# Denominators before numerators, and a fused bf16 weight, in a linear-attention kernel

## The chip, the cores and the metric

The kernel runs on one core of a Trainium2 chip. The metric is the device time in microseconds of one execution. TensorE multiplies matrices into PSUM banks of 512 fp32 columns; ScalarE and VectorE read PSUM and work in SBUF; SyncE (SP) issues DMAs; all engines run their own queues in program order and wait for each other by semaphores.

## The reference

The layer-normalised input (2048 tokens of 512, bf16) feeds two branches, whose sum is added to the input. The first is linear attention with 32 heads of 16:

```
phi = concat(softmax(p), softmax(-p))        # p = q @ w_phi or k @ w_phi, per head
kv  = sum over s of phi_k[s] (x) v[s];  z = sum over s of phi_k[s]
num = phi_q @ kv;  den = phi_q . z + 1e-6
branch_A = (num / den) @ wo
branch_B = mish(xn @ w1 + b1) @ w2           # 1792 hidden columns
out = x + branch_A + branch_B
```

## The kernel before

Tokens are worked in 16 tiles of 128, in groups of four. The first half of the program (to about 99 us) makes the layer norm, keys, values and the hidden layer; the second makes the query side, both second matmuls and the output. The order is written out by hand and kept, so each engine's queue is the program's order.

The query softmaxes are not normalised on their own: `exponentials` leaves exp of both signs ("planes") in `e`, and `turn` transposes it by DMA into `qT`. A pair h of two tiles then goes through these steps, i being the tile in the pair:

- `attend(h, i)` (L324) multiplies `qT` by the masked `kvm` in 32 small matmuls (L337) into `pnd`, four PSUM banks of which there is one set. For each of two planes and each head it holds 16 numerators, and for each pair of heads (a row block r and a column block j of 36 columns) four further columns: two denominators and two sums of the plane (the softmax denominators of the exponentials). ScalarE copies the numerators to SBUF as bf16 (L347; into the tiles `wkp` and `wv`, free by then) and the four columns as fp32 to `ds` (L348).
- `combine(h, parts)` (L350) works on VectorE on one tile (a slice of one) or both. It crosses each plane's denominator with the other plane's sum (`u`, L370), adds the two planes (`w`, L373), takes the reciprocal (L376), multiplies it by the other plane's sum to get each plane's weight (L379), and copies that to bf16 twice side by side (`f`, L382), because the product with the numerators (L389) then reads pairs of bf16. L396 adds the planes into `ob`, and L399 lets SP transpose it by DMA.
- `second_layer(t)` (L415) accumulates the second branch in `po`; `project_out(h)` (L424) adds the transposed `ob` times `wo` to the same bank, and `residual` (L432) adds the input and frees the bank.

The second half calls these steps interleaved, with `extremes` (L225 to L234: VectorE's maximum and minimum of each head), `exponentials` (L244, ScalarE) and `logits` (L168, copied at L209) of the next group between them. `combine` is called with single tiles for h = 0, 2, 3, 4 and 7, with both for h = 1, 5 and 6: 13 parts in all.

Of the kernel before, what the change touches and what calls it, by code (L numbers as in the profile page):

```python
# [10 lines left out]
FP32 = mybir.dt.float32  # L11

ACT = mybir.ActivationFunctionType
ALU = mybir.AluOpType
# [4 lines left out]
def kernel(  # L19
# [12 lines left out]
    nc = tc.nc  # L32
    P = 128
# [25 lines left out]
    opool = ctx.enter_context(tc.tile_pool(name="opool", bufs=2))  # L59
# [264 lines left out]
    def attend(h, i):  # L324

        if i == 0:
            nd_of[h] = (
                (wkp, wv)[h % 2][:].rearrange("p (i l) c -> p i l c", i=2),
                opool.tile([P, 2, 2, 4, 4, 4], FP32, name="ds"),
            )  # L330
        nm, ds = nd_of[h]
        pnd = later[0].tile([P, 4, 512], FP32, name="pnd", tag="nd")
        for pl in range(2):
            for j in range(4):
                for r in range(4):
                    at, rows = (pl * 4 + j) * 36, slice(32 * r, 32 * r + 32)
                    nc.tensor.matmul(  # L337
                        pnd[:, r, at : at + 36],
                        lhsT=qT_of[h][rows, i, pl * 4 + j, :],
                        rhs=kvm[rows, pl, j, :],  # L340
                        start=True,
                        stop=True,
                        tile_position=(32 * r, 0),
                    )
        a = pnd[:, :, 0:288].rearrange("p r (l j c) -> p l j r c", l=2, j=4)
        to = nm[:, i, :, :].rearrange("p l (j r c) -> p l j r c", j=4, r=4)
        nc.scalar.copy(to, a[:, :, :, :, 0:32])  # L347
        nc.scalar.copy(ds[:, i], a[:, :, :, :, 32:36])  # L348

    def combine(h, parts=(slice(0, 2),)):  # L350

        nm, ds = nd_of.pop(h) if parts[-1].stop == 2 else nd_of[h]
        ds = ds[:].rearrange("p i l j r (x h) -> p i l x (j r) h", x=2)
        if h not in oT_of:
            ob = lnp.tile([P, 4, 512], BF16, name="ob", tag="xn")
            u = opool.tile([P, 2, 2, 32], FP32, name="u")
            w = opool.tile([P, 2, 32], FP32, name="w")
            f = opool.tile([P, 2, 2, 32, 2], BF16, name="f")
            tmp_of[h] = ob[:, 0:2, :], u, w, f
            oT_of[h] = ob[:, 2:4, :].rearrange("p i (j c) -> p (i j) c", c=P)  # L360
        o_t, u, w, f = tmp_of[h]
        for q in parts:
            n = q.stop - q.start
            uh = u[:, q].rearrange("p i l (c h) -> p i l c h", h=2)
            wh = w[:, q, None, :].to_broadcast([P, n, 2, 32]).rearrange(
                "p i l (c h) -> p i l c h", h=2
            )
            for i in range(n):
                k = q.start + i
                nc.vector.tensor_tensor(  # L370
                    out=uh[:, i], in0=ds[:, k, :, 0], in1=ds[:, k, ::-1, 1], op=ALU.mult
                )
            nc.vector.tensor_tensor(  # L373
                out=w[:, q], in0=u[:, q, 0, :], in1=u[:, q, 1, :], op=ALU.add
            )
            nc.vector.reciprocal(w[:, q], w[:, q])  # L376
            for i in range(n):
                k = q.start + i
                nc.vector.tensor_tensor(  # L379
                    out=uh[:, i], in0=ds[:, k, ::-1, 1], in1=wh[:, i], op=ALU.mult  # L380
                )
            nc.vector.tensor_copy(  # L382
                f[:, q].rearrange("p i l c o -> p (i l c) o"),
                u[:, q].rearrange("p i l (c o) -> p (i l c) o", o=1).to_broadcast(
                    [P, n * 64, 2]
                ),
            )
            v = nm[:, q].rearrange("p i l (c e o) -> p (i l c) e o", e=8, o=2)
            nc.vector.tensor_tensor(  # L389
                out=v, in0=v,  # L390
                in1=f[:, q].rearrange("p i l c o -> p (i l c) o")[:, :, None, :].to_broadcast(
                    [P, n * 64, 8, 2]
                ),
                op=ALU.mult,
            )
            nc.vector.tensor_tensor(  # L396
                out=o_t[:, q], in0=nm[:, q, 0, :], in1=nm[:, q, 1, :], op=ALU.add
            )
            nc.sync.dma_start_transpose(  # L399
                out=oT_of[h][:, 4 * q.start : 4 * q.stop, :],  # L400
                in_=o_t[:, q].rearrange("p i c -> p (i c)"),
            )
# [55 lines left out]
    for sign in (1, -1):  # L458
        nc.gpsimd.affine_select(
            out=block[:], in_=block[:], pattern=[[-16 * sign, 8], [0, 16]],  # L460
# [9 lines left out]
    for _ in range(12):  # L470
# [7 lines left out]
        out=Wbd[:].rearrange("p j (h e) -> p j h e", h=8),  # L478
        in0=block[:, None, :, :].to_broadcast([P, 4, 8, 16]),
        in1=wsrc[:, :, None, :].to_broadcast([P, 4, 8, 16]),  # L480
        op=ALU.mult,
# [90 lines left out]
    hidden(2)  # L572
    second_layer(1, 0, 2)
    attend(0, 0)
    second_layer(1, 2, 12)
    attend(0, 1)
    extremes(5, halves=low)
    second_layer(1, 12)
    combine(0, first)
    combine(0, last)  # L580
    extremes(5, halves=high)
    exponentials(5, (0,))
    second_layer(2)
    attend(1, 0)
    second_layer(3)
    attend(1, 1)
    project_out(0)
    combine(1)
    store()
    for i in range(TPG):  # L590
# [92 lines left out]
```

## Time and profile before

| | |
|---|---|
| median of 3 runs | 181.95 us (181.59 to 182.17) |
| profiled execution | 181.76 us, span 179.8 us |
| granted TensorE clock | 0.997 |
| TensorE, VectorE, ScalarE busy | 170.8, 154.0, 123.9 us |
| numerators L347, denominators L348 (ScalarE) | 16 of 1.01 us, 16 of 0.27 us |
| `u` L370, `w` L373, reciprocal L376 (VectorE), one tile | 0.22, 0.19, 0.35 us |
| L379, `f` L382, L389, L396 (VectorE), one tile | 0.22, 0.23, 0.69, 0.42 us |
| DMA transposes of `ob` L399 | 13, median 2.5 us from issue to landing |

The span runs from the first instruction to the last; the rest of the execution's time lies around it. A wait is put down to whatever released the waiting instruction. A busy matmul is not a matmul at its peak: its end is modelled, so that matmuls are better counted by the pitch from one start to the next.

### The profile page before, as it was taken

The page shows a single profiled execution, that of the slowest core. Times are in us where ns is not written, and L with a number is a line of the kernel's source. Part 1 is how long each engine was busy: PE and PEld are TensorE (multiplying, and loading weights), DVE is VectorE, ACT ScalarE, POOL GpSimd, SP SyncE. Part 2 cuts the span into 40 slices and gives each one's busy share as a digit, 9 for nine tenths or more (in the row PEclk, how much of TensorE's full clock was granted, in tenths as well). Part 3 has the DMA queues.
Part 4 walks back from the last instruction along what each step waited for, and adds up shares of the span by engine and source line. Part 5 has one row for each costly group of instructions (what it writes and reads, how often), then busy time and mean ns, then how long its engine had stood idle before and what let it go on. Part 6 is the DMA issues. An engine that isn't in the chain of part 4 may idle for free.

```text
span 179.8 us, 4310 instructions
## 1 busy us (share of the span) xinstructions
PE 170.8 (95%) x1785; PEld 81.8 (46%) x1807; DVE 154.0 (86%) x313; ACT 123.9 (69%) x162; POOL 29.6 (16%) x42
## 2 busy tenths in 40 slices
PE   6799999999999999999999999899999999998993
PEld 2454443454444545544454444344444444443561
DVE  1989979997999989998999959799899978798853
ACT  2367999999998899969994987379223863543200
POOL 4404069400799300000000000000000000000000
PEclk9999999999999999999999999999999999999998
DMA  5997796300023600000000692809945078386334
GB/s 145 295 400 277 165 343 180 69 5 4 4 53 64 120 0 4 0 4 0 0 4 0 129 108 60 120 5 145 227 115 99 0 136 130 88 86 154 62 91 142
DMA packets 44527, 18.12 MB, mean 101 GB/s; under 512 B 36956, under 2 KB 43996, under 8 KB 44508
## 3 DMA queue, kind: packets, MB, share of 16 engines
q1 hardware_dynamic: 43536, 17.50, 44.4%
q10 hardware_dynamic: 972, 0.35, 0.7%
q8 instruction: 14, 0.23, 0.5%
q14 instruction: 5, 0.04, 0.1%
HBM read 6.84 MB, written 2.10 MB: 50 GB/s over the span
## 4 chain that ended last, share of the span: by engine, by line
DVE 47%; PE 33%; ACT 8%; DMA 8%; issue 2%; DVEq 0%; ACTq 0%; SPq 0%
PE po L415 14%; DVE s L262 7%; DVE m L225 6%; PE po L424 6%; PE ph L189 6%; PE pproj L168 5%; ACT e L244 5%; DVE stats L128 5%; DVE e L234 5%; DVE e L275 4%; DMA ob<-ob 4%; DVE r L270 3%; DMA qT<-e 2%; DVE x_sb L432 2%; DMA x_sb<-in_A_x_dram 2%
## 5 line engine op out<-in xcount | busy, mean ns | idle before, releaser
L415 PE MATMUL po<-w_sb,acts 128*128 128x512 bf16 (+1 forms) x224 | 50.2, 366 | 0.8 <-PE pnd L337 0.2
L189 PE MATMUL ph<-xnT,w_sb 128*128 128x512 bf16 x224 | 49.5, 379 | 0.4 <-ACT acts L196 0.4
L196 ACT ACTIVATE acts<-ph,b1f 128x512 bf16<-128x512 f32 x56 | 34.7, 705 | 2.0 <-PE ph L189 1.9
L244 ACT ACTIVATE e<-e 128x2048 bf16<-128x2048 bf16 x16 | 30.2, 1911 | 6.5 <-DVE e L234 6.4
L189 PEld LDWEIGHTS <-w_sb 128*128 128x128 bf16 x224 | 21.8, 98 | 26.8 <-issue 0.7
L415 PEld LDWEIGHTS <-acts 128*128 128x128 bf16 x238 | 22.2, 98 | 22.5
L168 PEld LDWEIGHTS <-xnT 128*128 128x128 bf16 x192 | 18.2, 98 | 22.0 <-DMA xnT<-xn 0.8
L262 DVE TENSOR_REDUCE s<-e 128x128 f32<-128x2048 bf16 x8 | 18.2, 2278 | 2.5 <-ACT e L244 2.5
L347 ACT CAST wv<-pnd 128x1024 bf16<-128x1024 f32 x8 | 8.1, 1010 | 14.5 <-PE pnd L337 12.3
L140 POOL TENSOR_SCALAR xn<-x_sb,mv,rstd 128x512 bf16<-128x512 bf16 x8 | 16.7, 2102 | 0.2
L424 PE MATMUL po<-wqk,ob 128*128 128x512 bf16 (+1 forms) x67 | 15.1, 367 | 1.3 <-DMA ob<-ob 1.2
L432 DVE TENSOR_TENSOR x_sb<-po,x_sb 128x512 bf16<-128x512 f32 (+1 forms) x17 | 11.0, 658 | 5.7 <-PE po L424 5.7
L168 PE MATMUL pproj<-wv,xnT 128*128 128x512 bf16 x61 | 14.8, 380 | 0.2
L209 ACT CAST p_sb<-pproj 128x512 bf16<-128x512 f32 x21 | 11.3, 587 | 4.9 <-PE pproj L168 4.9
L168 PE MATMUL pproj<-wqk,xnT 128*128 128x512 bf16 x62 | 14.4, 379 | 0.3 <-DVE x_sb L432 0.2
L225 DVE TENSOR_TENSOR m<-m 128x256 bf16<-128x256 bf16 (+2 forms) x44 | 13.4, 305 | 1.5
L128 DVE BATCH_NORM_STATS2 stats<-x_sb 128x6 f32<-128x512 bf16 x16 | 10.0, 680 | 3.8 <-DMA x_sb<-in_A_x_dram 3.8
L168 PE MATMUL pproj<-wkp,xnT 128*128 128x512 bf16 x50 | 11.8, 379 | 0.1
L347 ACT CAST wkp<-pnd 128x1024 bf16<-128x1024 f32 x8 | 8.1, 1014 | 3.5 <-PE pnd L337 3.4
L275 DVE TENSOR_TENSOR e<-e,r 128x2048 bf16<-128x2048 bf16 x8 | 10.3, 1282 | 0.3
L424 PEld LDWEIGHTS <-ob 128*128 128x128 bf16 x68 | 6.4, 98 | 8.3 <-DMA ob<-ob 1.8
L225 DVE TENSOR_TENSOR m<-p_sb 128x1024 bf16<-128x1024 bf16 (+1 forms) x18 | 10.2, 565 | 0.0
(66 smaller groups left out, 170.2 us busy)
## 6 DMA issues: line engine op xcount, KB each, us to landing
w_sb<-in_B_w_dram SPq DMA_DIRECT2D x2, 1792.0 KB, 8.9
out_dram<-x_sb SPq DMA_DIRECT2D x15, 128.0 KB, 1.9
x_sb<-in_A_x_dram SPq DMA_DIRECT2D x1, 1024.0 KB, 11.4
x_sb<-in_A_x_dram SPq DMA_DIRECT2D x1, 512.0 KB, 4.4
wv<-in_A_wqkv_dram SPq DMA_DIRECT2D x1, 512.0 KB, 5.2
wqk<-in_A_wo_dram SPq DMA_DIRECT2D x1, 512.0 KB
x_sb<-in_A_x_dram SPq DMA_DIRECT2D x1, 256.0 KB, 3.0
x_sb<-in_A_x_dram ACTq DMA_DIRECT2D x1, 256.0 KB, 3.3
```

The costliest lines, as they stand in the source:

```text
L128: nc.vector.bn_stats(stats[:, i, :], x_sb[:, t0 + i, :])
L140: engine.tensor_scalar(out=xn[:, at + i, :], in0=x_sb[:, t0 + i, :], scalar1=mv[:, i, 0:1], scalar2=rstd[:, i : i + 1], op0=ALU.subtract, ...
L168: nc.tensor.matmul(pp, lhsT=xnT[:, t, kt, :], rhs=w[:, kt, :], start=(kt == 0), stop=(kt == KT - 1),)
L189: nc.tensor.matmul(ph[:], lhsT=w1_sb[:, kt, f * P : (f + 1) * P], rhs=xnT[:, g * TPG : (g + 1) * TPG, kt, :], start=(kt == 0), stop=(kt == ...
L196: nc.scalar.activation(acts[:, f, g * 512 : (g + 1) * 512], ph[:], ACT.Mish, bias=b1f[:, f : f + 1])
L225: nc.vector.tensor_tensor(out=m, in0=src[:, :, 0:half], in1=src[:, :, half : 2 * half], op=op)
L244: nc.scalar.activation(v, v, ACT.Exp)
L262: nc.vector.reduce_sum(t[:], v.rearrange("p t l (c e) -> p (t l c) e", e=16), axis=AX.X)
L275: nc.vector.tensor_tensor(out=vv, in0=vv, in1=r2[:, :, None, :].to_broadcast([P, 128, 8, 2]), op=ALU.mult)
L347: nc.scalar.copy(to, a[:, :, :, :, 0:32])
L415: nc.tensor.matmul(po[:, c], lhsT=acts[:, f, t * P : (t + 1) * P], rhs=w2_sb[:, f, c], start=(f == 0), stop=False,)
L424: nc.tensor.matmul(po[:, c], lhsT=oT_of[h][:, t % 2 * 4 + j, :], rhs=wo_sb[:, j, c], start=False, stop=(j == 3),)
```

## The change

In `attend`, ScalarE copies the four columns first and the numerators second. The columns are laid out by plane of meaning: `ds` is now (tile, denominators or sums, 64), where it was (tile, plane, j, r, 4). In `combine`, `u` for two tiles is one instruction instead of two. The multiplication that gives each plane's weight writes bf16 pairs directly into `f`, reading both its fp32 operands with each element twice, one instruction for each tile; the separate copy into `f` is gone.

```
@@ attend
-                opool.tile([P, 2, 2, 4, 4, 4], FP32, name="ds"),
+                opool.tile([P, 2, 2, 64], FP32, name="ds"),
...
+        nc.scalar.copy(
+            ds[:, i].rearrange("p x (g r h) -> p g r x h", g=8, r=4),
+            pnd[:, :, 0:288].rearrange("p r (g c) -> p g r c", g=8)[:, :, :, 32:36].rearrange(
+                "p g r (x h) -> p g r x h", x=2
+            ),
+        )
         nc.scalar.copy(to, a[:, :, :, :, 0:32])
-        nc.scalar.copy(ds[:, i], a[:, :, :, :, 32:36])
@@ combine
-        ds = ds[:].rearrange("p i l j r (x h) -> p i l x (j r) h", x=2)
+        ds = ds[:].rearrange("p i x (l c) -> p i x l c", l=2)
...
-            for i in range(n):
-                k = q.start + i
-                nc.vector.tensor_tensor(
-                    out=uh[:, i], in0=ds[:, k, :, 0], in1=ds[:, k, ::-1, 1], op=ALU.mult
-                )
+            nc.vector.tensor_tensor(
+                out=u[:, q], in0=ds[:, q, 0], in1=ds[:, q, 1, ::-1], op=ALU.mult
+            )
             nc.vector.tensor_tensor(
                 out=w[:, q], in0=u[:, q, 0, :], in1=u[:, q, 1, :], op=ALU.add
             )
             nc.vector.reciprocal(w[:, q], w[:, q])
-            for i in range(n):
-                k = q.start + i
+            for k in range(q.start, q.stop):
                 nc.vector.tensor_tensor(
-                    out=uh[:, i], in0=ds[:, k, ::-1, 1], in1=wh[:, i], op=ALU.mult
+                    out=f[:, k],
+                    in0=ds[:, k, 1, ::-1, :, None].to_broadcast([P, 2, 32, 2]),
+                    in1=w[:, k, None, :, None].to_broadcast([P, 2, 32, 2]),
+                    op=ALU.mult,
                 )
-            nc.vector.tensor_copy(
-                f[:, q].rearrange("p i l c o -> p (i l c) o"),
-                u[:, q].rearrange("p i l (c o) -> p (i l c) o", o=1).to_broadcast(
-                    [P, n * 64, 2]
-                ),
-            )
```

## The prediction

> **What bounds the kernel now.** I read the page first: engine shares and the chain that ended last.
>
> ```profile
> PE 170.8 (95%) x1785; PEld 81.8 (46%) x1807; DVE 154.0 (86%) x313; ACT 123.9 (69%) x162; POOL 29.6 (16%) x42
> ...
> DVE 47%; PE 33%; ACT 8%; DMA 8%; issue 2%; DVEq 0%; ACTq 0%; SPq 0%
> ```
>
> TensorE is busy for 95% of the span, yet VectorE holds 47% of the chain. So the end is set by TensorE's list of matmuls plus the few places where that list waits, and a faster VectorE is worth only what those places lose. All instructions that the diff touches run after 102 us, so next I asked for the waits after 99 us (waiter, what it waited for: us in total, times, longest).
>
> ```profile
> DVE u L370 <- ACT ds L348: 2.3, 2, 1.9
> PEld L424 <- DMA ob<-ob: 1.8, 2, 1.1
> PE po L424 <- DMA ob<-ob: 1.2, 2, 0.6
> ...
> PE pproj L168 <- DVE x_sb L432: 0.2, 1, 0.2
> ```
>
> TensorE waits in the output projection (L424) for the transposed product twice, and once for a residual (L168 behind L432). The chain of waits shows how the first L424 wait comes about.
>
> ```profile
> 103.98 0.90 ACT wkp L347
> 104.88 0.18 ACT ds L348
> ...
> 106.47 0.70 DVE wkp L389
> ...
> 110.11 4.20 DMA ob<-ob
> 114.30 0.05 issue
> 114.35 1.04 PE po L424 x4
> ```
>
> ScalarE copies numerators, then denominators; VectorE, idle for 1.88 us by then, starts L370 at 105.08 and reaches L389 at 106.47, and from there to TensorE at 114.35 nothing else decides. The timeline gives the size of each wait and the two older chains.
>
> ```profile
> 112.70 1.04 PE L424 MATMUL po<-wqk,ob 128*128 128x512 bf16 x4
> 114.35 1.04 PE L424 MATMUL po<-wqk,ob 128*128 128x512 bf16 x4 [0.61 <-DMA ob<-ob]
> ...
> 136.26 3.61 PE L168 MATMUL pproj<-wqk,xnT 128*128 128x512 bf16 x16 [0.15 <-DVE x_sb L432]
> ...
> 158.94 0.36 DVE L379 TENSOR_TENSOR u<-ds,w 128x64 f32<-128x64 f32 x2
> ...
> 164.82 1.90 PE L424 MATMUL po<-wqk,ob 128*128 128x512 bf16 x8 [0.59 <-DMA ob<-ob]
> ```
>
> A busy matmul row includes its modelled tail, so I size waits by pitch. Undisturbed, 14 matmuls of 512 columns and one attend repeat every 3.43 us; 0.30 of that is the attend, so the pitch is 0.215 us. At 112.70 four matmuls end their slots at 113.56, and the next starts at 114.35: **0.79 us** lost. At 135.73 the first weights of L168 load, and undisturbed the matmul follows some 0.21 later; it starts at 136.26: **0.31 us** lost. At 163.85 an attend starts, 0.30 later L424 could; it starts at 164.82: **0.67 us** lost. Together 1.77 us.
>
> **The change, part by part.** *The copies' order.* ScalarE's pair costs the same: 1.01 and 0.27 us, the second starting about 0.15 before the first ends (104.76 against 103.87 + 1.01). The bank group pnd, of which there is one, is therefore released when it was, so the next attend does not wait longer. Denominators now end at about 103.87 + 0.27 = 104.14 instead of 105.05, numerators at about 105.04 instead of 104.88. The second is late only for whoever has nothing to do before needing them, and VectorE still has its chain ahead of L389: the added wait there is covered by that chain (1.19 us, below) against 0.90 us of numerators left. Without that cover it would cost at most 0.15 us.
>
> *The copy's layout.* The read order is as before, the writes now go in pairs of fp32 elements, the x planes 64 elements apart. No ScalarE row shows such a write. Lower bound 271 ns (L348 as it is; 1024 elements cost 1012, so time goes by the element, and a gain has nowhere to come from); upper bound twice that, 0.54 us. I take 0.27, because on VectorE the old L370 read in pairs at 218 ns, while L373 on 64 contiguous elements takes 225. At 0.54 the first chain below gains 1.02 instead of 1.29 us, still over what it needs.
>
> *VectorE, a part with one half (10 of 13).* Start to start in the first combine: u to w 0.26, w to reciprocal 0.23, reciprocal to u 0.38, u to f 0.26, f to L389 0.26: 1.39 us. The last two steps become one fp32 product of 128 elements. The trace has no such row: L373 costs 192 ns on 32 elements and 225 on 64, so 1.03 ns each, and 128 give 225 + 66 = 291. The floor is the cast's 227, the ceiling the reciprocal's slope (353 at 32, 554 at 64, 6.3 ns each), 0.96 us; it is a multiply with fp32 operands, so I take 0.29, with 0.03 to the next. The chain becomes 0.26 + 0.23 + 0.38 + 0.32 = 1.19 us: 0.20 saved.
>
> *A part with both halves (3 of 13).* In combine(5) L370 starts at 157.70, L373 at 158.09, L379 at 158.94, L389 at 159.66. One u on 128 elements takes 0.29 + 0.03, so 0.06 saved. The pair L379 takes 0.36 for two of 0.22, so the second adds 0.14; a pair of products of 0.29 then takes 0.29 + 0.21 + 0.03 = 0.53, against 0.72 from L379 to L389: 0.19 saved. Together 0.25 us.
>
> The Trainium skill ("VectorE: DVE Perf Modes", "The DRAIN you can't avoid") says the next instruction does not start until the pipe has emptied and that chaining doesn't avoid this, with earlier starts only for instructions that are not held. Taken strictly, the pair of products would cost 0.09 more and the whole sum below would be 1.2 us; the pair of 0.36 us for two of 0.22 is against it here.
>
> *Where it falls on the path.* Wait one: L389 of combine(0, first) moves from 106.47 to 104.19 + 1.19 = 105.38, 1.09 earlier (numerators are there at 105.04); the second part adds 0.20, so its transpose is issued 1.29 earlier, at 108.82, and lands near 113.0, before 113.56. All **0.79** are gained; late next is nothing, since the following residuals wait on TensorE itself. Wait two: VectorE runs without a gap from the residual at 127.55 through combine(2, last) and both parts of combine(3), so it is 0.6 earlier at the residual, which then waits for its matmuls: L424 at 134.21 plus the 1.06 that a residual follows at elsewhere (125.62 to 126.68) is 135.27 instead of 135.52: **0.25**. Wait three: the chain is residual at 157.09 (after TensorE), combine(5), transpose, L424; it shortens by **0.25** and stays the later one, with 0.42 left. The other combines have cover: their projections start with no wait. At the end, L424 runs through from 172.94 with no wait, so the tail gives nothing. SP issues the same transposes in the same order; the two qT transposes at 111.35, which queued behind ob's issue, move forward with it.
>
> Sum: 0.79 + 0.25 + 0.25 = 1.29 us. The profiled execution took 181.76 (span 179.8 and 1.96 around it), so 180.47; the median of the runs is 0.19 above it, so 180.66. I say 180.6.
>
> **Rivals.** *Only the first wait goes* (18%): waits two and three hang on residuals that follow TensorE and on a transpose that takes 3.08 us behind a qT transpose; if queueing eats the 0.25s, the gain is 0.79 and the time 181.15. For it: that landing is over the median of 2.5. Against it: qT there also follows VectorE's e, so it moves too.
>
> *Transposes land when the queue lets them* (12%): the first took 4.20 us, beside two qT transposes. If they fix its landing, the first gain is also lost: 181.7 to 181.95. Against it: qT's issue came after ob's, in order on SP.
>
> *The fused product is slow* (8%): two operands, each read twice over, one reversed by planes. Let it cost x more than 0.29. Then wait one gains 1.29 - 2x, at most 0.79; wait two 0.6 - 3x, at most 0.25; wait three 0.25 - 2x. The sum turns negative at x = 0.31, a product of 0.60 us; at the ceiling, x = 0.66, it is -0.03 - 1.38 - 1.07 = -2.5 us: 184.4. Against it: the cast L382 already repeats each element, at 227 ns.
>
> That the denominators do not come first cannot be, the queue being in program order.
>
> **How the numbers follow.** All three waits shrink: 62%, its own range 180.3 to 181.0 (0.35 either side of 180.66, half again the 0.25 of a smaller wait). A measurement here can tell about 0.3%, 0.55 us, from no change, so faster means under 181.40. The first case and nearly all of the second are: 0.79. Within: 0.14 (the third and the edge of the second). Slower: 0.07. The range runs from 180.1 (all 1.77 us of waits gone from the median, 180.18) to 181.7 (the second case, 181.15, with the 0.55 on top); the slow product and most of the third case lie outside.
>
> **What would show it.** Right: ds before the numerators, at 0.27 us; VectorE's idle before u at 104.2; a product near 0.29 us, and 1.19 from u to L389; no wait at the second L424 group, 0.4 us at the one near 164, none at L168 near 135; TensorE's idle after 99 us down by about 1.3. Wrong: a product over 0.6 us, a ds copy over 0.5, or transposes landing where they did though issued 1.3 earlier.

## The result and the profile after

The changed kernel takes 180.68 us (median of 6 runs, 180.49 to 180.89) against 182.12 for the kernel before beside it: ratio 0.9922, interval 0.9906 to 0.9939, so 1.44 us saved where 1.29 were forecast. The page of the changed kernel, engine shares and the chain that ended last (PEld is TensorE's weight load, a q behind an engine's name its instruction queue):

```profile
PE 171.7 (96%) x1785; PEld 82.3 (46%) x1807; DVE 151.9 (85%) x297; ACT 123.9 (69%) x162; POOL 29.6 (17%) x42
...
PE 47%; DVE 37%; ACT 8%; DMA 4%; issue 2%; POOL 0%; DVEq 0%; POOLq 0%; ACTq 0%; SPq 0%
```

VectorE has 16 instructions and 2.1 us fewer; its share of the chain fell by ten points, that of the transfers by four, and TensorE has them. Its waits after 98 us (same columns as before; L419 is the old L424):

```profile
DVE u L369 <- ACT ds L347: 1.0, 1, 1.0
...
PEld L419 <- DMA ob<-ob: 0.5, 1, 0.5
PE po L419 <- DMA ob<-ob: 0.4, 1, 0.4
```

Of the two waits for a transposed product one is left, and the wait of logits for a residual is off the list. The timeline shows the first chain and the places where TensorE used to wait:

```profile
104.25 0.27 ACT L347 COPY ds<-pnd 128x128 f32<-128x128 f32 x1
104.39 1.03 ACT L353 CAST wkp<-pnd 128x1024 bf16<-128x1024 f32 x1
104.55 0.23 DVE L369 TENSOR_TENSOR u<-ds 128x64 f32<-128x64 f32 x1 [0.97 <-ACT ds L347]
...
105.42 0.29 DVE L377 TENSOR_TENSOR f<-ds,w 128x128 bf16<-128x128 f32 x1
...
105.82 0.69 DVE L384 TENSOR_TENSOR wkp<-wkp,f 128x1024 bf16<-128x1024 bf16 x1
...
113.08 1.90 PE L419 MATMUL po<-wqk,ob 128*128 128x512 bf16 x8
...
158.23 0.49 DVE L377 TENSOR_TENSOR f<-ds,w 128x128 bf16<-128x128 f32 x2
...
164.00 1.90 PE L419 MATMUL po<-wqk,ob 128*128 128x512 bf16 x8 [0.41 <-DMA ob<-ob]
```

The eight matmuls at 113.08 run through: wait one is gone. A product costs 0.29 us, a pair 0.49. But from its start to L384 it is 0.40 us, not 0.32. In this trace all of the second half lies 0.33 us later to begin with (first attend at 102.77, not 102.44), so positions are compared relative to that.

Sized by pitch as in the prediction, the three waits were 0.79, 0.31 and 0.67 us (1.77) and are 0, 0.08 and 0.48 (0.56). These 1.21 us, less the later start, are the difference of the two traced executions (181.76 and 180.89). The other 0.2 us of the medians' 1.44 lie in executions that were not traced, and no run shows where.

### The profile page after: what moved, and what is told of

Read it like the earlier page. It is cut to its first block, busy times and chain, and to the rows that moved or that the text cites. A ratio compares the mean times of both kernels' runs of the same rounds, so it can differ in the third digit from the quotient of the medians.

```text
span 178.8 us, 4304 instructions
## 1 busy us (share of the span) xinstructions
PE 171.7 (96%) x1785; PEld 82.3 (46%) x1807; DVE 151.9 (85%) x297; ACT 123.9 (69%) x162; POOL 29.6 (17%) x42
## 4 chain that ended last, share of the span: by engine, by line
PE 47%; DVE 37%; ACT 8%; DMA 4%; issue 2%; POOL 0%; DVEq 0%; POOLq 0%; ACTq 0%; SPq 0%
PE po L410 21%; DVE s L262 7%; PE po L419 7%; DVE m L225 6%; PE ph L189 6%; PE pproj L168 5%; ACT e L244 5%; DVE e L234 5%; DVE e L275 4%; DVE stats L128 4%; DVE r L270 3%; PE warm L466 3%; PE pnd L337 2%; DMA qT<-e 2%; DMA ob<-ob 2%
## 5 line engine op out<-in xcount | busy, mean ns | idle before, releaser
L347 ACT COPY ds<-pnd 128x128 f32<-128x128 f32 x16 | 4.4, 275 | 18.0 <-PE pnd L337 15.7
L419 PE MATMUL po<-wqk,ob 128*128 128x512 bf16 (+1 forms) x67 | 14.9, 367 | 0.5 <-DMA ob<-ob 0.4
L419 PEld LDWEIGHTS <-ob 128*128 128x128 bf16 x68 | 6.5, 98 | 7.3 <-DMA ob<-ob 0.5
L234 DVE TENSOR_TENSOR e<-p_sb,m 128x2048 bf16<-128x2048 bf16 (+1 forms) x9 | 8.9, 989 | 0.3
```

Source lines behind the costliest of these rows:

```text
L234: nc.vector.tensor_tensor(out=e[:, :, pl, :].rearrange("p t (c e o) -> p t c e o", e=8, o=2), in0=p5 if pl == 0 else mb, in1=mb if pl == 0 ...
L419: nc.tensor.matmul(po[:, c], lhsT=oT_of[h][:, t % 2 * 4 + j, :], rhs=wo_sb[:, j, c], start=False, stop=(j == 3),)
```

## The experiments

One table first, then each run. Waits in us from each kernel's first trace, by the same pitch; two medians where a kernel was timed twice. The second traces give the same waits one and two, and 0.45 (changed), 0.34 (fuse_only) and 0.38 (first_pair) for wait three.

| kernel | wait one | two | three | median us | ratio to before (interval) |
|---|---|---|---|---|---|
| before, three traces | 0.79, 0.67, 0.96 | 0.31 | 0.67, 0.62, 0.61 | 181.95 to 182.34 | 1 |
| changed | 0 | 0.08 | 0.48 | 180.68, 180.66 | 0.9922 (0.9906-0.9939), 0.9926 (0.9908-0.9945) |
| order_only | 0 | 0.54 | 0.68 | 181.22 | 0.994 (0.9918-0.9962) |
| fuse_only | 0 | 0.08 | 0.39 | 180.53, 180.66 | 0.9906 (0.9886-0.9927), 0.9925 (0.9908-0.9942) |
| first_pair | 0 | 0.08 | 0.44 | 180.42, 180.43 | 0.9896 (0.9874-0.9918), 0.9913 (0.9896-0.9929) |
| product_twice | 0 | 0.92 | 1.07 | 182.09 | 0.9998 (0.9982-1.0013) |
| phase_shift | 0.11 | 0.31 | 0.62 | 181.49 | 0.9972 (0.9952-0.9992) |
| after_phase | 0 | 0.08 | 0.46 | 180.82 | 0.9933 (0.9914-0.9952) |
| split_five | 0 | 0.08 | 0 | 180.53 | 0.9909 (0.9894-0.9925) |

The three waits account for the traced times: from the first attend to the end of the span, less the three waits, all fourteen traces lie between 75.4 and 75.7 us. What else differs between them is when the first attend starts, 102.42 to 102.79 us, and 103.79 in after_phase.

**The order alone.** Before's kernel, two lines exchanged:

```
+        nc.scalar.copy(ds[:, i], a[:, :, :, :, 32:36])
         nc.scalar.copy(to, a[:, :, :, :, 0:32])
-        nc.scalar.copy(ds[:, i], a[:, :, :, :, 32:36])
```

> Only the order of ScalarE's two copies is changed, layout and VectorE's instructions are those of before. Theory of the three waits: VectorE starts 0.9 us earlier in the first combine, but L389 now has a wait of its own for the numerators, 0.08 us for each part. Wait one (second group of the first output projection) falls from 0.79 to about 0 (0 to 0.1), wait two grows from 0.31 to about 0.5 (three parts), wait three from 0.67 to about 0.75: sum -0.4 to -0.5 us against before. Rival, that the time follows VectorE's busy time wherever it lies: VectorE does the same work, so no change (0.0). Second rival, that the added wait costs nothing: -0.8 us.

The traced execution took 181.22 us, 0.54 less than the traced one of before, a little over the first theory's sum; waits one and two came out as expected, wait three at 0.68 instead of about 0.75. The group of L389 (durations in ns, least, median and longest) shows where the added wait sits, the timeline what it does:

```profile
L389 DVEq EVENT_SEMAPHORE  x13: 21/21/326, 105.6 to 170.8; - x13
```

```profile
135.77 3.61 PE L168 MATMUL pproj<-wqk,xnT 128*128 128x512 bf16 x16 [0.37 <-DVE x_sb L432]
...
164.35 1.90 PE L424 MATMUL po<-wqk,ob 128*128 128x512 bf16 x8 [0.61 <-DMA ob<-ob]
```

L389 now waits for numerators as well as for `f`; the numerators' wait is an instruction of its own on VectorE's queue, 13 times instead of once, and the gap between `f` and L389 grows from 0.03 to 0.10 us. Wait two grows from 0.31 to 0.54 by it; wait three is hardly longer. In the medians the gain is 1.1 us (0.7 to 1.5 by the interval), more than the traces say, and there the second rival's 0.8 would do as well: what speaks against it is wait two. More on the medians below.

**The fusion alone.** The changed kernel with the numerators' copy ahead of the other:

```
+        nc.scalar.copy(to, a[:, :, :, :, 0:32])
         nc.scalar.copy(
             ds[:, i].rearrange("p x (g r h) -> p g r x h", g=8, r=4),
...
         )
-        nc.scalar.copy(to, a[:, :, :, :, 0:32])
```

> The layout by plane and the fused product of the changed kernel, but numerators are copied first, as before. Theory of the three waits: L389's numerators are older than the denominators, so no added wait, the gap from product to L389 is 0.03 and a one-tile part saves 0.20 us. Wait one keeps 0.79 - 0.40 = 0.4 us, wait two falls by 0.25, wait three by 0.25: sum -0.9 us against before, 0.3 to 0.5 slower than the changed kernel. Rival (VectorE's busy time): the full gain of the changed kernel, -1.4 us, since it has all the saved work.

A miss for the first theory: 1.3 to 1.8 us faster than before, not 0.9. Its chain came out as expected:

```profile
105.99 0.29 DVE L377 TENSOR_TENSOR f<-ds,w 128x128 bf16<-128x128 f32 x1
106.32 0.69 DVE L384 TENSOR_TENSOR wkp<-wkp,f 128x1024 bf16<-128x1024 bf16 x1
...
112.74 1.90 PE L419 MATMUL po<-wqk,ob 128*128 128x512 bf16 x8
```

Product to L384 is 0.33 without the added wait. But wait one is gone altogether, though the transpose is issued only 0.3 us earlier than before (109.8 against 110.1). The same transpose in before and here, from issue to landing:

```profile
L399 SPq DMA_TRANSPOSE ob<-ob x1: 1190/1190/1190, 110.1 to 110.1; - x1
DMA to landing us min/median/max: 4.2/4.2/4.2
```

```profile
L394 SPq DMA_TRANSPOSE ob<-ob x1: 1191/1191/1191, 109.8 to 109.8; - x1
DMA to landing us min/median/max: 2.4/2.4/2.4
```

So 4.2 us was not the time of this transpose but an accident to it. A transpose leaves 16 landing events in the trace, called marks here, and they say which (us; q8 and q14 are the transfers nearest to it on two instruction queues, of 16 and 8 KB; fuse_again is a second trace of fuse_only):

```
kernel        issued  marks by 113.2  last mark  q8 from  q14 from
before        110.1   15 of 16        114.30     112.47   111.96
before_again  110.3   15              114.36     112.53   112.33
before_third  110.2   14              114.61     112.25   112.26
phase_shift   110.4   15              113.92     110.39   112.22
order_only    109.4   16              111.99     112.12   110.07
fuse_only     109.8   16              112.16     112.67   118.21
fuse_again    110.1   16              112.57     112.52   118.57
changed       109.3   16              111.75     113.47   118.47
```

In before, 15 marks were there by 112.55, in time for the matmuls at 113.56; one came at 114.30, after the two instruction transfers. fuse_again tells the two transfers apart. Its transpose is issued when before's is, its qT transposes follow at the same times (111.4 and 112.7 us) and its 16 KB transfer starts where before's does; only the 8 KB one is away, and all 16 marks are in by 112.57:

```profile
q8 instruction: 1, 0.02, 2.2%
...
qT<-e SPq DMA_TRANSPOSE x2, 4.1
ob<-ob SPq DMA_TRANSPOSE x1, 2.4
```

So neither the larger transfer alone nor the qT transposes hold it up.

**Denominators first only where VectorE waits for them.** The changed kernel, and in `attend`:

```
+        if h > 0:
+            nc.scalar.copy(to, a[:, :, :, :, 0:32])
         nc.scalar.copy(
             ds[:, i].rearrange("p x (g r h) -> p g r x h", g=8, r=4),
...
         )
-        nc.scalar.copy(to, a[:, :, :, :, 0:32])
+        if h == 0:
+            nc.scalar.copy(to, a[:, :, :, :, 0:32])
```

> The changed kernel, with denominators first only in the two attends of the first pair; elsewhere numerators first. Theory: wait one is still gone, the added wait of 0.08 us is gone from 11 of 13 parts, so wait three falls from 0.48 to about 0.42, wait two stays at the 0.08 that its residual sets: 0.05 to 0.1 us faster than the changed kernel, within what this measurement tells; in the trace, product to L384 0.32 us start to start instead of 0.40 from the second pair on. Rival, that denominators first is worth something in later pairs too: slower than the changed kernel by 0.2 us or more.

It has the lowest median each time, 0.23 us under the changed kernel where the two ran side by side, but their ranges overlap. The rival falls: denominators first is worth nothing in later pairs. From the product to L387 (the old L389) it is 0.33 from the third pair on (128.31 to 128.64).

**A dose of the slow product.**

```
-            for k in range(q.start, q.stop):
+            for k in [k for k in range(q.start, q.stop) for _ in range(2)]:
```

> The changed kernel with the fused product issued twice for each tile, writing the same values; this gives the slow product of the prediction a dose of about 0.3 us for each tile. Theory of the three waits: chain one gains 0.93 - 2 x 0.32 = 0.3 to 0.5 of the 0.79, wait two, whose chain had 0.36 to give, grows by 3 x (0.32 - 0.12) = 0.6, wait three grows by 2 x 0.2 to 0.32 less the 0.2 saved, so by 0.2 to 0.4: sum about +0.3 to +0.6 us against before, that is some 1.7 us slower than the changed kernel, of 16 x 0.32 = 5 us of added VectorE work. Rival (VectorE's busy time sets the time): +3 us or more against before. Rival (VectorE has slack everywhere but in wait one): no slower than before.

```profile
105.10 0.62 DVE L377 TENSOR_TENSOR f<-ds,w 128x128 bf16<-128x128 f32 x2
```

```profile
136.13 3.61 PE L168 MATMUL pproj<-wqk,xnT 128*128 128x512 bf16 x16 [0.76 <-DVE x_sb L427]
...
165.11 1.90 PE L419 MATMUL po<-wqk,ob 128*128 128x512 bf16 x8 [1.00 <-DMA ob<-ob]
```

Waits two and three grew by 0.61 and 0.40 over before, as expected. Wait one, of which 0.3 to 0.5 us were to remain, did not come back: the transpose was issued 0.4 us before the old time and not held up. So the time is that of before and not the 0.3 to 0.6 us above it that were expected, at a product of 0.62 us, where the prediction's point of no gain was 0.60. The 16 further products, 5 us of VectorE's time, cost 1.4 us against the changed kernel. The first rival, 3 us over before, is out. The second named the right time, no slower than before, for a wrong reason: VectorE has no slack ahead of waits two and three, which grew.

**The collision by itself.** Before's kernel, and the changed one (after_phase), with 42 instructions more on TensorE's queue at the start (21 matmuls, each with its weight load):

```
-    for _ in range(12):
+    for _ in range(9):
         nc.tensor.matmul(
...
+    for _ in range(24):
+        nc.tensor.matmul(warm[:, 0:16], lhsT=ident[:], rhs=ident[:, 0:16], start=True, stop=True)
```

> The kernel before, with three of its twelve warm-up matmuls replaced by 24 of 16 columns: 42 instructions more on TensorE, before its first real work. Nothing near the change is touched. Theory of the collision: in the trace of before, 15 of 16 landing marks of the transpose of combine(0, last) are there at 112.55, the last at 114.30, after an instruction-queue transfer of 16 KB that starts at 112.47; with more instructions ahead the transfer comes some 2 us earlier, and the transpose lands 2.4 to 3.2 us after its issue, so wait one is gone without any change to VectorE or ScalarE: 0.6 to 1.2 us faster than before. Rival (the chain of the prediction: the landing of 4.2 us is the transposes' own queueing): no change to wait one, within 0.2 us of before.

> The changed kernel with the same 42 further instructions on TensorE. Theory of the collision: its transpose is issued 0.8 us earlier and is not hit in either phase, so no gain at wait one: within 0.3 us of the changed kernel, up to 0.4 faster if wait three (behind qT transposes held up near 158) shortens too. Rival, that the warm-up's form itself is worth something: the same gain here as in the kernel before.

The DMA queues between 111 and 114.5 us, before and phase_shift (packets, MB, share of 16 engines):

```profile
q8 instruction: 1, 0.02, 1.7%
q14 instruction: 1, 0.01, 0.7%
```

```profile
q14 instruction: 1, 0.01, 0.8%
```

```profile
112.99 2.02 PE L424 MATMUL po<-wqk,ob 128*128 128x512 bf16 x8
```

The 16 KB transfer starts 2 us earlier, and with nothing changed on VectorE or ScalarE wait one falls to 0.11 us (the eight matmuls take 2.02 us where undisturbed ones take 1.90). The median is 0.73 us below before's 182.22; by the ratio's interval the gain lies between 0.1 and 0.9. The changed kernel gains nothing (0.9933 against 0.9922 and 0.9926). The times are a poor measure here, because in some executions the first half runs later, probably by the shorter warm-up: in after_phase's trace the first 16 matmuls behind it (L110) take 1.89 us instead of 1.07 in phase_shift's, the second half starts 1.0 us later than in the changed kernel, and this execution, with the changed kernel's waits, took 181.90 us, which none of its runs exceeds. Five of phase_shift's twelve runs took over 182.1; whether for the same reason, no trace shows.

The last mark is still 0.8 us behind the others, with the 8 KB transfer in the same stretch. The Trainium skill ("Runtime: NRT & Kernel Launch", "Instruction fetch mechanics") says that each engine's sequencer fetches blocks of 16 KiB, 256 instructions, on a DMA queue of its own, at a cost that is mostly hidden. That 42 more TensorE instructions moved q8's 16 KB transfer agrees; q14's transfers are of 8 KB here. From the transpose in flight the fetches were not hidden: its last mark came 0.8 to 1.95 us late.

q14 follows VectorE's instructions: it starts at 112.0 to 112.3 in the four traces with before's VectorE code, at 110.1 in order_only with its 12 more waits, and at 117.6 to 119.5 in every fused kernel that issues its product once. That it is VectorE's queue is inferred from this. So fuse_again escapes because VectorE's 16 instructions fewer put off this transfer; the changed kernel's transpose has landed by 111.75 and might escape by that alone. The larger transfer alone costs nothing (fuse_again), nor does the smaller early in the flight (order_only, product_twice); both together cost 1.6 to 1.95 us, and the smaller at 112.2 with the larger ahead of it 0.8. How they delay a mark, and what the smaller would do alone at 112, no run shows.

**Before, traced twice more.** The same program.

> The kernel before, profiled once more. Theory of the collision: the instruction-queue transfer near 112.5 starts up to 0.5 us earlier or later than in the first trace, and wait one, 0.79 us there, comes out different by 0.2 us or more, with the transposes issued at the same time. Rival (chain): wait one is 0.79 us again within 0.1.

> A third trace of the kernel before. Theory of the collision: the last of 16 landing marks of the transpose of combine(0, last) comes 1.5 us or more behind the others again, and wait one lies anywhere from 0.3 to 1.3 us. Rival (chain): all marks come together near 112.6 at times, and then the run takes under 181.2 us.

Wait one was 0.67 and 0.96 us, the executions 181.83 and 182.06; each time one or two marks were late by 1.6 us or more. The first expectation, a difference of 0.2 or more, was missed at 0.12, and so was its rival's 0.1; the third trace was 0.17 off. What the chain theory cannot explain is the marks. Before's medians in four sets of runs (181.95 to 182.34) lie up to 0.6 us above its traced executions (181.76, 181.83, 182.06). So part of what the other kernels gain in the medians is time that untraced executions of before lose; where, no run shows.

**The last wait.** first_pair, and:

```
-    combine(5)
+    combine(5, first)
+    combine(5, last)
```

> The kernel with denominators first in the first pair alone, and combine(5) called for its two tiles one after the other, each with its own transpose. Theory of the waits: the first transpose is issued near 159.1 and lands before 163.2, the second near 161.4 and lands near 163.8, before its matmuls at 164.1, so wait three falls from 0.44 to between 0 and 0.3 us: 0.1 to 0.4 us faster than without the split. Rival: the 0.8 us more of VectorE's work delays combine(6) and the residuals behind it, and the bank for the last second layer comes late: 0.2 to 0.6 us slower.

Weight loads and matmuls at the old place of wait three:

```profile
163.45 0.55 PEld L422 LDWEIGHTS <-ob 128*128 128x128 bf16 x4
164.31 0.56 PEld L422 LDWEIGHTS <-ob 128*128 128x128 bf16 x4 [0.31 <-DMA ob<-ob]
```

```profile
165.81 1.46 PE L413 MATMUL po<-w_sb,acts 128*128 128x512 bf16 x6 [0.15 <-DVE x_sb L430]
```

0.86 between the two groups is four slots of 0.215: wait three is gone. But half of it is lost again behind it: TensorE is there before VectorE's residual has freed the bank, and the next second layer starts 0.52 us after its attend instead of 0.30. Both theories hold in part, and the time is that of first_pair (180.53 against 180.42).

**Side by side.** The changed kernel and the two variants again, on one chip.

> The changed kernel once more, beside the two variants on the same chip. By the waits in its trace (0.08 and 0.48 us left of the three), 1.2 us faster than the traced run of before; since the kernel before is traced at 181.8 but has a higher median, 1.2 to 1.8 us in the medians.

> Denominators first in the first pair alone, once more. Waits left: 0.08 and 0.44 us. Theory of the waits: 0 to 0.15 us faster than the changed kernel on the same chip. Rival (denominators first pays in later pairs): slower by 0.2 us or more.

> Numerators first everywhere, layout and fused product of the changed kernel, once more. Waits left: 0.08 and 0.39 us. Theory of the waits with the collision: the change of order is worth nothing once the product is fused, so 0 to 0.2 us faster than the changed kernel. Rival (the prediction's chain, in which the order gives 0.4 us of wait one that the fusion can't): slower by 0.3 us or more.

They take 180.66, 180.43 and 180.66 us. With the product fused, the order of the copies is worth nothing that can be measured; the prediction's chain, in which order gave what fusion could not, is refuted here.

## Why the prediction was right, step by step

- **What bounds the kernel.** Right: the time follows TensorE's three waits, not VectorE's busy time. order_only gains with VectorE's work unchanged; product_twice adds 5 us of it for 1.4. The pitch of 0.215 us is right (single starts lie 0.216 apart), but not by the division given: (3.43 - 0.30)/14 is 0.224, the period holding a gap of 0.1 ahead of each attend. No wait changes by more than 0.04 for it.
- **ScalarE's pair.** Right: ds costs 0.274 us in its new layout (0.271 before), starts first, and VectorE's idle time in front of it fell from 1.88 to 0.97 us.
- **The product.** Right at 0.291, and 0.49 for a pair, as two overlapping instructions give; one after the other they would have taken 0.58.
- **The chain of 1.19 us.** Mis-sized: 1.27 for one tile, 1.76 from L369 to L384 for two (forecast 1.71). The prediction asked whether the added wait would last, found it covered, and left out that it is itself an instruction in the queue, 0.07 us for each part.
- **Wait one, 0.79.** Right in size, wrong in its reason. The step that failed is "its transpose is issued 1.29 earlier, at 108.82, and lands near 113.0": it carried 4.20 us of landing along as if it were the transpose's own time. It was 2.4, and the rest a hold-up beside instruction transfers; the rival on landing times looked at the same number and blamed qT. The issue moved by 0.8 us only (1.1 relative to the first attend), and no earlier issue was needed once VectorE's instruction transfer lay elsewhere: fuse_again issues at 110.1 as before and loses nothing. That the forecast time came out although the landing was misread is partly luck.
- **Wait two, 0.25.** Right: 0.23. The 0.08 left is the same in every fused kernel that issues its product once, so TensorE's own matmuls set it, as the prediction said.
- **Wait three, 0.25.** 0.19; without the added wait it was 0.28 (fuse_only). Before's own three traces lie 0.06 apart.
- **The slow product.** Its point of no gain, 0.60 us, was close to the dose of 0.62 that gave no gain, partly by luck: by its formula wait one should have kept 0.16 us and wait two grown by 0.39; wait one was gone and wait two grew by 0.61.

## What to carry to other kernels

Where one engine is busy for 95%, size its waits by the pitch of its instructions and cost a change by those alone. When a transfer on the path lands much later than its like, look at each of its landing events before carrying the delay along in a sum. A wait that is already met when it is reached can still cost an instruction on the waiting queue: 0.07 us here, 13 times. An experiment at the start of a program can shift all that follows: measure from a point behind the edit as well.

## What the runs showed of the hardware that was not expected

A transpose whose 15 other landing marks were in by 112.55 ended at 114.30 when transfers of 16 and 8 KB for the instruction queues started at 112.47 and 111.96; with the larger moved 2 us away, its last mark was 0.8 us late instead of 1.75, and with the smaller away and the larger in place (112.52) none was late. So 42 instructions at the start of one queue took 0.68 us off a wait some 110 us later, and 16 fewer on VectorE (q14 being its queue, as inferred above) took it away: code that is shorter or longer moves such collisions about.
